# Attention's P V product: the part with v's low half is added into the columns of the high half, and a pair's part is normalised in its PSUM bank

## The chip, the cores and the metric

The kernel runs on one core of a Trainium2 chip. Its engines are TensorE (PE, with its weight loads shown apart as PEld), VectorE (DVE), ScalarE (ACT), GpSimd (POOL) and the issuing queues of SyncE (SP) and ACT for DMAs. The metric is the device time of one execution in microseconds, lower is better; the time before is the median of three runs.

## The reference

Three layers follow each other, all from float32 arrays (weights and inputs are sent as 64-bit numbers and decoded on the chip).

```python
# q, k, v: (4 batches, 8 heads, 576 rows, 64)
q_rot, k_rot = rotate(q), rotate(k)                    # rotary embedding
scores = q_rot @ k_rot^T / 8
attn = exp(scores - rowmax);  attn /= attn.sum + 1e-9
x = (attn @ v), heads side by side                     # (2304, 512)
h = x @ w_in;  x = (h * clip(h + 3, 0, 6) / 6) @ w_out # layer 1, 512 -> 2048 -> 512
h = x @ w2_in; x = (P(h) / Q(h)) @ w2_out              # layer 2, a rational function
```

## The kernel before

Products are made exact enough by splitting a float32 operand into a high and a low half-precision part (layer 2 splits into two float32r parts) and adding the three larger of the four part products.

**Attention.** A batch has eight heads, taken as four pairs (P = 4 b + p). A pair's 576 rows are cut into 128-row chunks 0 to 3 for each head and one chunk 4 of 64 rows of both heads: nine chunks a pair, 36 a batch, 144 in all. They are ordered by batch, then by part: part 0 holds chunks 0 and 1 of all four pairs (16 chunks), part 1 chunks 2, 3 and 4 of all four pairs (20 chunks). For one chunk, `chunk` writes these steps: scores on PE (line 762, PSUM tile `s`), row maximum on DVE (766), its scaling on DVE or POOL (767), exponential on ACT (772, tile `e`), the high half of P (776) and the low half (779, 780) into tile `p` (three buffers), a DMA transpose on SP's queue into `pt` (784, three buffers), and then the product with v on PE (792).

v's tile `v9` of a pair has for each of five row blocks the high half with a column of ones beside it (65 columns, z = 0) and the low half with a column of zeros (65 columns, z = 1). A product is nine matmuls: the five blocks with P's high half (four and the last, shared one) take all 130 columns, the four blocks with P's low half only the first 65. The 64-row chunk does this once for each head. So the result in PSUM has a high part and a low part side by side. Its place is one of the two banks `ob0` and `ob1`, by turns from chunk to chunk. DVE adds the two parts (lines 801 and 804, a reduction over two) into the SBUF tile `xua` (part 0) or `xub` (part 1).

When a pair's part is complete, `x_out` normalises it: a sum with 1e-9 and a reciprocal on DVE (817, 818), the multiply (820, tile `xn`) on POOL or DVE as the planner chooses, the split into `xh` and `xl` (824, 825), and two DMA transposes into `xt` (828), the input of layer 1.

The banks' other columns hold small results (`small`, column 264 or 392 on): sums of squares for scaling, by turns in the two banks. One of them is the transpose of v's maxima in `scale_v` (line 663), which starts the scaling of a batch's v: a maximum (665), a matmul with ones (667), and `pow2` (524, 526, 528), and then `prep_v` writes v's high half (679, on POOL or ACT) and low half (681, DVE).

**Layer 1** (`layer1`) is called for each batch and part. Its 16 hidden blocks (line 859) and four output tiles (line 883) take PSUM tiles `h` from a ring of two; each output tile is copied out by ACT. **Layer 2** starts when attention is over. Its weights are decoded earlier, in the gaps of attention (`prep_w2`).

**What sets the order.** Nothing is issued as it is written. Each step is an `op` with the engines it may run on, an estimated cost, the tiles that it reads and writes, and a priority in ticks (one chunk is a tick; the table `PR` shifts each kind of step). `Plan.order` goes through planned time, and at each moment gives each free engine the ready step of the highest priority; the order that comes out is what each engine gets, and an engine takes its instructions in that order. Tiles with one tag form a ring: they are used in the order in which they were made,

```python
            for n, t in enumerate(ts):
                o = t.ops[0]
                if n:
                    first.append((ts[n - 1].ops[0], o))
                if n >= t.bufs:
                    for x in t.ops:
                        x.deps.update(y for y in ts[n - t.bufs].ops if y is not x)
```

so the first step on a tile comes after the first step on the tile before it, and after all steps on the tile whose buffer it takes. The main loop writes the chunks of a batch in order; after chunk (4, 0) of each pair it calls `scale_v` (at the first pair), `prep_qk` and `prep_v` of the next batch, and after the last pair of a part `layer1` of that part.

Of the kernel before, what the change touches and what calls it, by code (L numbers as in the profile page):

```python
# [10 lines left out]
F32 = mybir.dt.float32  # L11
# [5 lines left out]
ALU = mybir.AluOpType  # L17
AX = mybir.AxisListType
# [5 lines left out]
D = 64  # L24
D2 = 2 * (D + 1)
HP = 4
NB = 9
# [5 lines left out]
LSH = 7  # L33
# [206 lines left out]
def two(e):  # L240
    return float(2.0 ** e)
# [167 lines left out]
def c_dve(n, ap=0):  # L409
    return n * 1.042 + 68 + 60 * ap  # L410
# [27 lines left out]
def attention_moe_moe2(ctx, tc, q, k, v, w1i, w1o, w2i, w2o, a, b, tabs, out):  # L438
# [4 lines left out]
    vec, act, pool, pe, sp = nc.vector, nc.scalar, nc.gpsimd, nc.tensor, nc.sync  # L443
    DE = {"Q": sp, "A": act}
    EL = {"D": vec, "G": pool, "A": act}
# [12 lines left out]
    op, tl = pl.op, pl.tile  # L458

    def EN(key):  # L460
        return PR.get(key + "0", PR[key]) if pl.early else PR[key]
# [25 lines left out]
    obank = [tl("psa", [128, 512], F32, f"ob{i}") for i in range(2)]  # L487
    xu0 = [tl("attn", [128, 2, 2, D + 1], F32, f"xua{i}") for i in range(2)]
    xu1 = [tl("attn", [128, 3, 2, D + 1], F32, f"xub{i}") for i in range(2)]
# [12 lines left out]
    for i in range(2):  # L502
        op("D", 140, lambda e, i=i: vec.memset(xu1[i]()[64:128, 2], 0.0), w=[(xu1[i], "0")])
# [5 lines left out]
    def small(m, n, kind=0):  # L509

        i = nsmall[kind]
        nsmall[kind] += 1
        c = 264 + kind * 128
        t = obank[i % 2]
        return (t, c), lambda: t()[0:m, c:c + n]
# [133 lines left out]
    def scale_v(b_):  # L649
# [10 lines left out]
        for p in range(HP):  # L660
            bound((am, p), lambda p=p: am()[:, p:p + 1], t, 640, 1.4143, lambda p=p: t()[:, 2 * p:2 * p + 2])
        ps, ps_ap = small(HP, 128)
# [5 lines left out]
           r=[ones, m4], w=[p2])  # L668
# [77 lines left out]
    def chunk(i):  # L746
        P, part, cc, h, n = order[i]
        qt, kt, k2, al = prep[P]
        v9 = v9s[P]
        s = tl("psa", [128, 1024], F32, "s", 2)  # L750
# [5 lines left out]
        def mm(e):  # L756
# [12 lines left out]
           r=[(mx, 0), (al, 1)], w=[(mx, 1)])  # L769
        et = tl("attn", [128, S], F32, "e", PR["e"])  # L770
        c0 = cc - 2 * part
# [11 lines left out]
        pt = tl("attn", [128, NB, 128], F16, "pt", PR["pt"])  # L783
        op("Q", (625, 1008, 1), lambda e: DE[e].dma_start_transpose(out=pt(), in_=p16()), r=[p16], w=[pt])
        ob = obank[i % 2]
        vs = [(h, 0, 128, 0)] if cc < 4 else [(0, 0, 64, 0), (1, 64, 64, D2)]

        def pv(e):
            for hh, q0, m, o0 in vs:
                for n_, j in enumerate((0, 1, 2, 3, 5, 6, 7, 8, 4)):  # L790
                    c = D2 // 2 if j > 4 else D2
                    pe.matmul(ob()[0:m, o0:o0 + c], lhsT=pt()[:, j, q0:q0 + m],  # L792
                              rhs=v9()[:, hh, j % 5].rearrange("p s d -> p (s d)")[:, 0:c],
                              start=(n_ == 0), stop=(n_ == NB - 1))
        pl.prio += PR["pv"] * PR["tick"]
        op("P", (c_pe(D2, 5) + c_pe(D + 1, 4)) * len(vs), pv, r=[pt, v9], w=[(ob, 0)])
        xu = (xu0, xu1)[part][n % 2]

        def ev(e):
            if cc < 4:  # L800
                vec.tensor_reduce(out=xu()[:, c0, h], in_=ob()[:, 0:D2].rearrange("p (s d) -> p d s", s=2),
                                  axis=AX.X, op=ALU.add)
            else:
                vec.tensor_reduce(out=xu()[0:64, c0],
                                  in_=ob()[0:64, 0:2 * D2].rearrange("p (h s d) -> p h d s", h=2, s=2),
                                  axis=AX.X, op=ALU.add)
        op("D", c_dve(128 * len(vs)), ev, r=[(ob, 0)], w=[(xu, (c0, h))])

    def x_out(P, part, n):

        b_, p = divmod(P, HP)
        m = 2 + part
        if p == 0:
            xts[b_, part] = [tl("attn", [128, HP, m * 128], F16, f"xt{part}{i}") for i in range(2)]
        xu = (xu0, xu1)[part][n % 2]
        r = tl("attn", [128, 3, 2], F32, "r", 2)
        op("D", 75, lambda e: vec.tensor_scalar(r()[:, 0:m], xu()[:, :, :, D], 1e-9 * two(LSH), None, ALU.add), r=[xu], w=[r])
        op("D", 105, lambda e: vec.reciprocal(r()[:, 0:m], r()[:, 0:m]), w=[r])
        xn = tl("attn", [128, 3, 2, D], F32, "xn")
        op(EN("e_xn"), {"G": 1.75 * m * 128 + 125, "D": c_dve(m * 128)}, lambda e: EL[e].tensor_tensor(  # L820
            xn()[:, 0:m], xu()[:, :, :, 0:D], r()[:, 0:m].unsqueeze(3).to_broadcast([128, m, 2, D]), ALU.mult), r=[xu, r], w=[xn])
# [357 lines left out]
```

## Time and profile before

| | us |
|---|---|
| median of 3 runs (lowest, highest) | 1174.5 (1174.15, 1177.13) |
| the profiled execution | 1176.04 |
| its span, first to last instruction | 1174.3 |
| DVE busy | 1012.9 |
| PE busy | 978.5 |
| ACT busy | 693.6 |
| POOL busy | 536.2 |

The span is what the trace covers; the execution's own time is a little longer. The first product with v starts at 75.3 us and the last at 696.6 us, layer 1 goes on to 762 us, and layer 2 fills the rest. A busy time is the union of an engine's instructions, and the matmuls' ends are modelled: a matmul is shown for about 0.2 us, while the next one starts much earlier. Which engine limits a stretch is read from the stretch, not from the sums.

### The profile page before, as it was taken

The numbers are of one execution on the slowest core, as the hardware profiler recorded it, in microseconds if no ns is written. First come the engines' busy times: TensorE is split into PE (matmuls) and PEld (weight loads), VectorE is DVE, ScalarE is ACT, GpSimd is POOL, SyncE is SP. The second block draws the span as 40 slices with busy tenths as digits, with TensorE's granted clock in tenths as the row PEclk, the third lists the DMA queues.
The fourth block names the chain that finished last, engine by engine and source line by source line (L and its number), as shares of the span: only waits on it lengthen the run. The fifth ranks groups of instructions, "written<-read, shape, count | busy, mean of one in ns | idle before, by whom it ended". The sixth has DMA issues, their size and how long they took to land.

```text
span 1174.3 us, 20041 instructions
## 1 busy us (share of the span) xinstructions
PE 978.5 (83%) x7030; PEld 756.6 (64%) x7030; DVE 1012.9 (86%) x1920; ACT 693.6 (59%) x1274; POOL 536.2 (46%) x603
## 2 busy tenths in 40 slices
PE   0222469887888889988899999989999999999997
PEld 0111247755566666666666787767888888888885
DVE  7999989799899998899978955489988887888787
ACT  5555668475455354453444526478776675676576
POOL 5799778687588857699843620035000000000000
PEclk9999989999999999899999999999999999999999
DMA  8788877787887897978869651622020020010010
GB/s 237 184 219 178 218 145 156 152 175 163 189 177 157 154 220 187 191 149 161 188 165 196 145 127 33 197 83 76 1 61 3 19 54 1 5 41 1 1 37 18
DMA packets 297445, 142.73 MB, mean 122 GB/s; under 512 B 245120, under 2 KB 278528, under 8 KB 297344
## 3 DMA queue, kind: packets, MB, share of 16 engines
q1 hardware_dynamic: 286352, 123.72, 48.8%
q10 hardware_dynamic: 10992, 17.73, 5.3%
q8 instruction: 55, 0.90, 0.3%
q14 instruction: 46, 0.38, 0.1%
HBM read 61.71 MB, written 17.83 MB: 68 GB/s over the span
## 4 chain that ended last, share of the span: by engine, by line
PE 42%; DVE 28%; DMA 8%; issue 6%; POOL 6%; ACT 4%; SPq 1%; ACTq 0%; DVEq 0%; POOLq 0%
PE ac L1079 14%; PE hh L1046 8%; PE hx L1046 7%; PE h L883 6%; PE h L859 5%; DMA pt<-p 4%; DVE mx L766 3%; DVE gl L868 2%; DVE p L453 2%; DVE t L865 2%; DMA w2d<-f 2%; DMA raw<-in_moe_w_out_dram 2%; DVE qk L732 1%; ACT e L772 1%; PE s L762 1%
## 5 line engine op out<-in xcount | busy, mean ns | idle before, releaser
L859 PE MATMUL h<-xt,w 128*128 128x256 f16 (+1 forms) x1536 | 207.6, 289 | 31.8 <-DVE t L865 27.4
L859 PEld LDWEIGHTS <-w 128*128 128x128 f16 x1536 | 149.2, 99 | 73.9 <-issue 36.9
L883 PE MATMUL h<-gh,w 128*128 128x256 f16 (+1 forms) x960 | 195.8, 290 | 0.5 <-DVE w L574 0.4
L772 ACT ACTIVATE e<-s,mx,qal 128x576 f32<-128x576 f32 x144 | 118.7, 827 | 122.8 <-DVE mx L767 37.5
L1079 PE MATMUL ac<-w,lgh 128*128 128x512 f32 x576 | 180.1, 393 | 4.8 <-ACT lgh L1069 4.0
L779 POOL TENSOR_TENSOR p<-e,p 128x512 f16<-128x512 f32 x104 | 138.9, 1335 | 64.6 <-DVE p L453 42.5
L883 PEld LDWEIGHTS <-w 128*128 128x128 f16 x1440 | 139.5, 99 | 36.3 <-DVE w L574 0.7
L883 PE MATMUL h<-gl,w 128*128 128x256 f16 (+1 forms) x480 | 139.2, 290 | 0.0
L762 PE MATMUL s<-t,t 128*128 128x512 f16 (+2 forms) x320 | 89.6, 313 | 55.1 <-ACT e L772 48.2
L792 PE MATMUL ob<-v,pt 128*128 128x130 f16 (+3 forms) x1440 | 96.3, 217 | 45.2 <-DMA pt<-p 19.3
L762 PEld LDWEIGHTS <-t 128*128 128x128 f16 (+1 forms) x640 | 59.0, 108 | 107.2 <-issue 68.4
L1079 PEld LDWEIGHTS ac<-w,lgh 128*128 128x128 f32 x576 | 106.8, 188 | 30.6 <-ACT lgh L1069 6.6
L1046 PE MATMUL hh<-x,w 128*128 128x512 f32 (+1 forms) x516 | 115.9, 373 | 2.9 <-DVE lt L1061 2.9
L792 PEld LDWEIGHTS <-pt 128*128 128x128 f16 (+1 forms) x1440 | 81.5, 105 | 55.4 <-issue 26.4
L1079 PE MATMUL ac<-w,lgl 128*128 128x512 f32 x288 | 113.6, 394 | 1.2 <-DVE lgl L1070 1.2
L766 DVE TENSOR_REDUCE mx<-s 128x1 f32<-128x576 f32 x144 | 107.0, 745 | 6.8 <-PE s L762 6.6
L1046 PEld LDWEIGHTS hh<-x,w 128*128 128x128 f32 x516 | 90.9, 188 | 23.0 <-DVE lt L1061 3.8
L1046 PE MATMUL hx<-x,w 128*128 128x512 f32 (+1 forms) x444 | 98.2, 370 | 0.0
L863 ACT ACTIVATE t<-h,half,d 128x256 f32<-128x256 f32 (+1 forms) x128 | 74.7, 585 | 26.9 <-PE h L859 25.7
L1046 PEld LDWEIGHTS hx<-x,w 128*128 128x128 f32 x444 | 77.4, 188 | 16.1
L868 DVE TENSOR_TENSOR gl<-t,gh 128x256 f16<-128x256 f32 (+1 forms) x108 | 69.2, 643 | 12.1 <-ACT gh L449 11.0
L449 ACT ACTIVATE gh<-t 128x256 f16<-128x256 f32 (+1 forms) x95 | 41.6, 440 | 51.1 <-DVE t L865 48.8
(151 smaller groups left out, 2088.8 us busy)
## 6 DMA issues: line engine op xcount, KB each, us to landing
raw<-in_moe_w_in_dram SPq DMA_DIRECT2D x32, 512.0 KB, 4.8
raw<-in_moe_w_out_dram SPq DMA_DIRECT2D x32, 512.0 KB, 4.5
w2d<-f ACTq DMA_DIRECT2D x30, 256.0 KB, 3.7
w2s<-w2d SPq DMA_DIRECT2D x22, 256.0 KB, 2.7
out_dram<-ob SPq DMA_DIRECT2D x36, 128.0 KB, 2.4
nat<-in_k_dram SPq DMA_DIRECT2D x16, 256.0 KB, 3.2
nat<-in_q_dram SPq DMA_DIRECT2D x16, 256.0 KB, 3.2
vnat<-in_v_dram SPq DMA_DIRECT2D x4, 1024.0 KB, 7.6
```

The source lines that it names most:

```text
L449: act.activation(out, in_, AF.Copy, scale=scale)
L762: pe.matmul(s()[r0:r0 + m, c:c + n_], lhsT=qq[:, q0:q0 + m], rhs=kk[:, k0:k0 + n_], start=(j == 0), stop=(j == 1))
L766: op("D", c_dve(576), lambda e: vec.reduce_max(mx()[:, 0:1], s()[:, 0:S], axis=AX.X), r=[s], w=[(mx, 0)])
L772: op("A", c_act(576, 2, False), lambda e: act.activation(et(), s()[:, 0:S], AF.Exp, bias=mx()[:, 1:2], scale=al()[:, 0:1]), r=[s, (mx, 1), ...
L779: EL[e].tensor_tensor(p16()[:, S + 64:2 * S], et()[:, 0:512], p16()[:, 0:512], ALU.subtract)
L792: pe.matmul(ob()[0:m, o0:o0 + c], lhsT=pt()[:, j, q0:q0 + m], rhs=v9()[:, hh, j % 5].rearrange("p s d -> p (s d)")[:, 0:c], start=(n_ == 0 ...
L859: pe.matmul(hp()[:, 0:N], lhsT=w[:, z, kk], rhs=xt()[:, kk, 0:N], start=(n == 0), stop=(n == 11))
L863: op("A", c_act(N, 2, False), lambda e, t=t, hp=hp, f=f: act.activation(t()[:, 0:N], hp()[:, 0:N], AF.Relu, bias=half(), scale=d()[:, f:f ...
L868: op(EN("e_gl"), c_sub(N), lambda e, t=t, f=f: EL[e].tensor_tensor(gl()[:, f, 0:N], t()[:, 0:N], gh()[:, f, 0:N], ALU.subtract), r=[t, (gh ...
L883: pe.matmul(yp()[:, 0:N], lhsT=w[:, s_, m * 128:(m + 1) * 128], rhs=gt()[:, f, 0:N], start=(f == 0 and z == 0), stop=(f == KF - 1 and z == 2))
L1046: pe.matmul(hp()[:, 0:n], lhsT=w[:, kk], rhs=xt()[:, kk, 0:n], start=(i == 0), stop=(i == 11))
L1079: pe.matmul(accs[j][i]()[0:m], lhsT=gt()[:, x:x + m], rhs=wt(), start=(f == 0 and z == 0), stop=(f == KF - 1 and z == 2))
```

## The change

The product's matmuls with v's low half get their own instruction, 64 columns wide, and write to the columns of the high half, so that PSUM adds the two: 14 narrow matmuls (five blocks twice, four blocks once) in place of nine. The bank is chosen by part (2 P + part is odd for part 1) instead of by chunk, and each chunk and head of a pair's part has its own 65 columns in it, up to 390. The two reductions and their SBUF tiles are gone. `x_out` reads the sums and the values from the bank; its multiply is now given to DVE only. Rows 64 to 127 of the 64-row chunk's columns, which no product writes, are set to 1 once. The small results move to columns 400 and 464 on; the transpose of v's maxima, 128 columns wide, takes a tile of layer 1's ring `h`.

```diff
--- before.py
+++ after.py
@@ -485,8 +485,6 @@
     pw = tl("const", [128, 3], F32, "pw")
     pwi = tl("const", [128, KF], F32, "pwi")
     obank = [tl("psa", [128, 512], F32, f"ob{i}") for i in range(2)]
-    xu0 = [tl("attn", [128, 2, 2, D + 1], F32, f"xua{i}") for i in range(2)]
-    xu1 = [tl("attn", [128, 3, 2, D + 1], F32, f"xub{i}") for i in range(2)]
     v9t = [tl("attn", [128, 2, 5, 2, D + 1], F16, f"v9{i}") for i in range(HP)]
 
     def cosb():
@@ -500,7 +498,7 @@
     op("D", 140, lambda e: vec.memset(ones(), 1.0), w=[ones])
     op("D", 70, lambda e: vec.memset(half(), two(-16)), w=[half])
     for i in range(2):
-        op("D", 140, lambda e, i=i: vec.memset(xu1[i]()[64:128, 2], 0.0), w=[(xu1[i], "0")])
+        op("D", 140, lambda e, i=i: vec.memset(obank[i]()[64:128, 4 * (D + 1):6 * (D + 1)], 1.0), w=[(obank[i], 0)])
     for i in range(HP):
         for z, x in enumerate((1.0, 0.0)):
             op("D", 70, lambda e, i=i, z=z, x=x: vec.memset(v9t[i]()[:, :, :, z, D:D + 1], x), w=[(v9t[i], f"1{z}")])
@@ -510,7 +508,7 @@
 
         i = nsmall[kind]
         nsmall[kind] += 1
-        c = 264 + kind * 128
+        c = 400 + kind * 64
         t = obank[i % 2]
         return (t, c), lambda: t()[0:m, c:c + n]
 
@@ -659,7 +657,10 @@
         op(PR["q_vnat"], (1700, 4300), load, w=[t])
         for p in range(HP):
             bound((am, p), lambda p=p: am()[:, p:p + 1], t, 640, 1.4143, lambda p=p: t()[:, 2 * p:2 * p + 2])
-        ps, ps_ap = small(HP, 128)
+        ps = tl("psh", [128, 512], F32, "h", 2)
+
+        def ps_ap():
+            return ps()[0:HP, 0:128]
         op("P", 110, lambda e: pe.transpose(ps_ap(), am(), ident()), r=[ident] + [(am, p) for p in range(HP)], w=[ps])
         m4 = tl("attn", [HP, 1], F32, "vm4", 2)
         op("D", 200, lambda e: vec.reduce_max(m4(), ps_ap(), axis=AX.X), r=[ps], w=[m4])
@@ -782,29 +783,17 @@
         op(en, {"D": 740, "G": 1380}, lo, r=[et, (p16, 0)], w=[(p16, 1)])
         pt = tl("attn", [128, NB, 128], F16, "pt", PR["pt"])
         op("Q", (625, 1008, 1), lambda e: DE[e].dma_start_transpose(out=pt(), in_=p16()), r=[p16], w=[pt])
-        ob = obank[i % 2]
-        vs = [(h, 0, 128, 0)] if cc < 4 else [(0, 0, 64, 0), (1, 64, 64, D2)]
+        ob = obank[(2 * P + part) % 2]
+        vs = [(h, 0, 128, (2 * c0 + h) * (D + 1))] if cc < 4 else [(0, 0, 64, 4 * (D + 1)), (1, 64, 64, 5 * (D + 1))]
 
         def pv(e):
             for hh, q0, m, o0 in vs:
                 for n_, j in enumerate((0, 1, 2, 3, 5, 6, 7, 8, 4)):
-                    c = D2 // 2 if j > 4 else D2
-                    pe.matmul(ob()[0:m, o0:o0 + c], lhsT=pt()[:, j, q0:q0 + m],
-                              rhs=v9()[:, hh, j % 5].rearrange("p s d -> p (s d)")[:, 0:c],
-                              start=(n_ == 0), stop=(n_ == NB - 1))
+                    for z in range(2 if j < 5 else 1):
+                        pe.matmul(ob()[0:m, o0:o0 + D + 1 - z], lhsT=pt()[:, j, q0:q0 + m], rhs=v9()[:, hh, j % 5, z, 0:D + 1 - z],
+                                  start=(n_ == 0 and z == 0), stop=(n_ == NB - 1 and z == 1))
         pl.prio += PR["pv"] * PR["tick"]
         op("P", (c_pe(D2, 5) + c_pe(D + 1, 4)) * len(vs), pv, r=[pt, v9], w=[(ob, 0)])
-        xu = (xu0, xu1)[part][n % 2]
-
-        def ev(e):
-            if cc < 4:
-                vec.tensor_reduce(out=xu()[:, c0, h], in_=ob()[:, 0:D2].rearrange("p (s d) -> p d s", s=2),
-                                  axis=AX.X, op=ALU.add)
-            else:
-                vec.tensor_reduce(out=xu()[0:64, c0],
-                                  in_=ob()[0:64, 0:2 * D2].rearrange("p (h s d) -> p h d s", h=2, s=2),
-                                  axis=AX.X, op=ALU.add)
-        op("D", c_dve(128 * len(vs)), ev, r=[(ob, 0)], w=[(xu, (c0, h))])
 
     def x_out(P, part, n):
 
@@ -812,13 +801,16 @@
         m = 2 + part
         if p == 0:
             xts[b_, part] = [tl("attn", [128, HP, m * 128], F16, f"xt{part}{i}") for i in range(2)]
-        xu = (xu0, xu1)[part][n % 2]
+        ob = obank[(2 * P + part) % 2]
+
+        def ov():
+            return ob()[:, 0:2 * m * (D + 1)].rearrange("p (j h d) -> p j h d", j=m, h=2)
         r = tl("attn", [128, 3, 2], F32, "r", 2)
-        op("D", 75, lambda e: vec.tensor_scalar(r()[:, 0:m], xu()[:, :, :, D], 1e-9 * two(LSH), None, ALU.add), r=[xu], w=[r])
+        op("D", 75, lambda e: vec.tensor_scalar(r()[:, 0:m], ov()[:, :, :, D], 1e-9 * two(LSH), None, ALU.add), r=[(ob, 0)], w=[r])
         op("D", 105, lambda e: vec.reciprocal(r()[:, 0:m], r()[:, 0:m]), w=[r])
         xn = tl("attn", [128, 3, 2, D], F32, "xn")
-        op(EN("e_xn"), {"G": 1.75 * m * 128 + 125, "D": c_dve(m * 128)}, lambda e: EL[e].tensor_tensor(
-            xn()[:, 0:m], xu()[:, :, :, 0:D], r()[:, 0:m].unsqueeze(3).to_broadcast([128, m, 2, D]), ALU.mult), r=[xu, r], w=[xn])
+        op("D", {"D": c_dve(m * 128)}, lambda e: vec.tensor_tensor(
+            xn()[:, 0:m], ov()[:, :, :, 0:D], r()[:, 0:m].unsqueeze(3).to_broadcast([128, m, 2, D]), ALU.mult), r=[(ob, 0), r], w=[xn])
         xh = tl("attn", [128, 3, 2, D], F16, "xh")
         xl = tl("attn", [128, 3, 2, D], F16, "xl")
         op(EN("e_xh"), c_copy(m * 128), lambda e: copy(e, xh()[:, 0:m], xn()[:, 0:m]), r=[xn], w=[xh])
```

## Rows read from the trace of the kernel before

**Rows 1.** The page: span, and busy time, share and instructions of each engine.
```profile
span 1174.3 us, 20041 instructions
...
PE 978.5 (83%) x7030; PEld 756.6 (64%) x7030; DVE 1012.9 (86%) x1920; ACT 693.6 (59%) x1274; POOL 536.2 (46%) x603
```

**Rows 2.** Busy us of each engine by stretch; x is instructions, then clock, DMA.
```profile
60.00:580.00 520.00, 394.92 (x3649) 294.50 (x3648) 484.99 (x963) 284.71 (x527) 414.02 (x477) 0.98 0.83 175
580.00:700.00 120.00, 113.21 (x1097) 87.59 (x1097) 97.86 (x230) 53.32 (x92) 56.06 (x70) 0.99 0.74 164
700.00:770.00 70.00, 68.43 (x479) 50.81 (x477) 31.99 (x59) 37.85 (x68) 1.75 (x2) 1.00 0.35 111
```

**Rows 3.** Chain of waits: by engine over the span; by line after 700 us.
```profile
PE 42%; DVE 28%; DMA 8%; issue 6%; POOL 6%; ACT 4%; SPq 1%; ACTq 0%; DVEq 0%; POOLq 0%
...
by line: PE ac L1079 34.9%; PE hh L1046 18.6%; PE hx L1046 16.5%; PE h L883 6.5%; PE h L859 5.5%; DVE lt L1068 2.4%; DVE lt L1066 2.2%; DVE lq L1058 2.1%; DVE lq L1065 2.0%; DVE lgl L1070 1.6%; DVE lt L1060 1.4%; issue 1.4%; DVE lt L1061 0.
```

**Rows 4.** Groups by line and shape: count | busy us, mean ns | idle before.
```profile
L801 DVE TENSOR_REDUCE xua<-ob 128x65 f32<-128x130 f32 x64 | 18.0, 282 | 3.3 <-PE ob L792 3.0
L801 DVE TENSOR_REDUCE xub<-ob 128x65 f32<-128x130 f32 x64 | 17.8, 279 | 2.0 <-PE ob L792 2.0
L804 DVE TENSOR_REDUCE xub<-ob 64x130 f32<-64x260 f32 x16 | 6.6, 411 | 4.6 <-PE ob L792 4.6
L820 POOL TENSOR_TENSOR xn<-xub,r 128x384 f32<-128x384 f32 x14 | 13.6, 972 | 8.7 <-DVE r L818 8.6
L820 POOL TENSOR_TENSOR xn<-xua,r 128x256 f32<-128x256 f32 x9 | 7.2, 804 | 11.9 <-DVE r L818 11.1 <-ACT w L449 0.6
L865 DVE SCALAR_TENSOR_TENSOR t<-t,h 128x256 f32<-128x256 f32 x64 | 26.0, 407 | 0.7 <-ACT t L863 0.6
```

**Rows 5.** PE in order of time: start us, us shown, matmuls merged.
```profile
434.55 0.57 PE L792 MATMUL ob<-v,pt 128*128 128x130 f16 x9
434.96 3.60 PE L859 MATMUL h<-xt,w 128*128 128x320 f16 x24
...
445.12 0.19 PE L762 MATMUL s<-t,t 128*128 128x64 f16 x1
445.15 0.19 PE L762 MATMUL s<-k,t 128*128 128x64 f16 x1
```

**Rows 6.** Waits from 60 to 700 us: total us, times, longest us.
```profile
PE ob L792 <- DMA pt<-p: 19.3, 16, 3.0
PE ob L792 <- DVE xua L801: 4.0, 2, 2.3
...
SPq L784 <- PE ob L792: 37.9, 28, 5.2
```

**Rows 7.** In order of time: first and last bank hand-over of the 24.
```profile
88.19 0.26 DVE L801 TENSOR_REDUCE xua<-ob 128x65 f32<-128x130 f32 x1
...
96.58 0.68 PE L792 MATMUL ob<-v,pt 128*128 128x130 f16 x5
...
684.92 0.41 DVE L804 TENSOR_REDUCE xub<-ob 64x130 f32<-64x260 f32 x1
684.93 0.57 PE L792 MATMUL ob<-v,pt 128*128 128x130 f16 x9
685.60 0.15 DVE L817 TENSOR_SCALAR r<-xub 128x6 f32<-128x6 f32 x1
...
686.90 0.54 DVE L820 TENSOR_TENSOR xn<-xub,r 128x384 f32<-128x384 f32 x1
```

**Rows 8.** PE in order of time around batch 2's first product.
```profile
315.06 0.27 PE L663 MATMUL ob<-ident,vam 128*4 128x128 f32 x1
...
396.31 0.58 PE L792 MATMUL ob<-v,pt 128*128 128x130 f16 x9 [1.24 <-DMA pt<-p]
...
400.72 0.27 PE L883 MATMUL h<-gh,w_s 128*128 128x256 f16 x1
```

## The prediction

> **What bounds the kernel now.** I read the page's first part, then the busy time by stretches of the span, then the chain of waits, then the single instructions that the change touches. The page says that VectorE (DVE) is the busiest engine, 86% of the span against 83% for TensorE (PE) [rows 1]. An average over the span hides that there are two halves. By stretches [rows 2], from 60 to 580 us DVE is busy 485.0 of 520 us (93%) while PE is busy 394.9 (76%); from 580 to 700 us PE is busy 113.2 of 120 (94%) and DVE 97.9; from 700 us on PE has 68.4 of 70, and there is no attention work left. So attention, which is all that the change touches, runs where DVE is fullest, and hands over to a stretch where PE is.
>
> The chain of waits puts 28% of the span on DVE, 329 us of 1174.3; after 700 us DVE's lines add up to 2.4 + 2.2 + 2.1 + 2.0 + 1.6 + 1.4 = 11.7% of 474 us, 55 us [rows 3]. That leaves 274 us of chain on DVE up to 700 us. DVE is busy 485.0 + 97.9 = 583 us between 60 and 700. Of a DVE microsecond in attention about 274/583 = 0.47 lies on the chain. The rest is beside other work.
>
> **The change part by part.** *The reductions go.* 128 of them over one head and 16 over the 64-row chunk cost 18.0 + 17.8 + 6.6 = 42.4 us of DVE [rows 4]. All lie before 700 us.
>
> *The normalising multiply goes to DVE.* The edit names DVE alone, where the planner chose between GpSimd (POOL) and DVE; 23 of the 32 are on POOL now, 14 of 384 and 9 of 256 elements, 13.6 + 7.2 = 20.8 us of POOL [rows 4]. On DVE the 384-element one took 0.54 us from SBUF [rows 7]. None reads PSUM here; the nearest row that does is line 865, 256 elements with one operand in PSUM, 0.41 us [rows 4], so I take the SBUF price for PSUM. DVE gains 14 x 0.54 + 9 x 0.41 = 11.3 us. From the other side, if each cost what POOL takes now, it would be 20.8. The sum and the reciprocal ahead of it stay on DVE; the sum reads four or six PSUM elements instead of SBUF ones, bounded by 0 and by a whole reduction more, 0.28 x 32 = 9 us; I take nothing, since its element count is far below the reduction's 130.
>
> DVE's net: 42.4 - 11.3 = 31 us less. At 0.47 that is 14.6 us of the chain; bounds 0 (all hidden) and 31 (DVE sets the pace throughout). I take 14.
>
> *PE runs 14 matmuls instead of 9 in each product*, 800 more in all, with 800 more weight loads. A group of nine starts at 434.55 and the next group at 434.96 [rows 5]: 0.41 us. Two 64-wide matmuls of line 762, each with its own weight load, start 445.12 and 445.15, 0.03 us apart [rows 5]. So four 65-wide ones are 0.12 us, the five 130-wide ones 0.29 or 0.058 each, and 14 narrow ones 14 x 0.03 = 0.42: the same as now. Times 160 groups, 1.6 us, taken as nothing. The upper bound is a group whose 14 steps all take 0.058, 0.81 us, or 64 us more of PE; the lower is a gain of some 3 us. The cover is PE's idle 125 us before 580; after that there is none.
>
> The Trainium skill, "TensorE: Matmul & The Clock Gate", section "LDWEIGHTS (loading the stationary operand)", speaks against this: it gives a weight load as its columns over 1.2, 107 ns for 128, and "Back-to-back issue gap" says that both instructions of a pair set the spacing. By an estimate from that page five more pairs a group would be 0.53 us, 85 us of PE. The trace does not agree for these shapes: nine pairs in 0.41 us.
>
> *The bank is handed over.* A batch's four pairs of one part now follow each other in the same bank, where chunks alternated between two. Inside a pair nothing waits any more: the next chunk has its own columns. But the first product of the next pair waits for sum, reciprocal and multiply of the one before. There are 32 such ends; 8 change part and so bank, 24 do not. The last of the 24 [rows 7]: DVE reads the product at 684.92, sums at 685.60, and ends the multiply at 687.44, 1.84 us after the sum began; with the reduction gone the sum takes its place, and the multiply ends at 686.76. The next product began at 684.93, so it is 1.8 us late. The first of the 24 goes the other way: reduction at 88.19, next product at 96.58 [rows 7], no wait. Worked like this, 12 of the 24 are late, by some 1.5 us each: 18 us of late products. Queued behind a waiting product on PE is a layer-1 group or the next scores, and behind those ACT's exponentials; its transposed P stays in its buffer, and the transposes on SP's queue stand behind that: they wait for products 37.9 us now, 28 times [rows 6].
>
> What speaks for a small price: the same kind of wait stands in the kernel today (a product waits for the reduction two chunks back), 142 times, and PE stood still for it only twice, 4.0 us [rows 6], because the order written out by the planner puts other matmuls ahead. I take 5 us, with 0 and 18 as ends. On DVE the waiting read becomes rarer: 32 sums wait for a product, not 144 reductions.
>
> *v's maximum moves into the ring of layer 1's PSUM tiles.* Tiles of a ring are used in the order in which they are made. scale_v of the next batch is called at the end of the first pair of part 1, after layer 1 of part 0 was laid out, so its transpose can only come after the fourth output tile of that layer 1 has begun and the third is copied out. For batch 2 it now runs at 315.06; that fourth tile begins at 400.72, and the batch's first product was at 396.31 [rows 8]. From the transpose on there are seven steps on PE, DVE and POOL (maximum, sum, three small ones, v's high half, v's low half), each behind a running instruction (DVE's average is 583/1193 = 0.49 us, POOL's 470/547 = 0.86 [rows 2]), two of them about 1 us themselves: an estimate of 8 to 9 us. So the first product comes at about 410, 14 us late; batch 3 repeats this, somewhat milder (11), batch 1 has slack. The scores, exponentials and splits don't need v: a chunk takes 640/144 = 4.4 us, so 14 us is three chunks, and three buffers of split P and three of transposed P can hold them. I take 3 us for both together; the ends are 0 and 25.
>
> *The rest* is free: two memsets change their place at the start, the small results move to other columns, and two tiles leave SBUF.
>
> The sum: -14 + 5 + 3 + 0 = -6 us. The profiled execution took 1176.0 us, 1.7 beyond its span; it becomes 1170.0. It was 1.5 above the median of the runs, 1174.5, so the median becomes 1168.5. The planner works out the whole order anew, so each engine's order from 60 to 700 us can shift; that has no row, and the ranges hold it.
>
> **The rivals.** *All of the 31 us comes through*: DVE at 93% from 60 to 580 speaks for it; against it PE's 94% after 580, and that only 0.47 of DVE's time is on the chain. With the two small waits hidden: about 1174.5 - 25 = 1150.
>
> *The relief is hidden anyway*: what is late next is PE waiting for transposed P, 19.3 us today [rows 6], and the full PE after 580. A faster DVE then waits for both; 1174.
>
> *The hand-over decides (slower).* PE is in order. If the planned place of a next pair's product is right after the multiply, any lateness of DVE stops PE with everything behind it. The price: 18 us of late products, and as much again where late products hold transposed P and SP's queue, less the 14: +22, less what overlaps, about 1185. It decides as soon as a hand-over costs more than 14/24 = 0.6 us on average. For it: DVE is nearly full, so sum, reciprocal and multiply each queue. Against it: PE's 4.0 us now.
>
> *Late v decides (slower).* If the pipeline ahead of the products is full already, batches 2 and 3 lose the whole 14 and 11 us: -14 + 5 + 25 = +16, about 1190. Against it the six buffers.
>
> *Weight loads set the pace (slower).* 64 us of PE, half of it uncovered: 1200. The skill's figure above would make it more; the rows speak against it.
>
> **How the numbers follow.** Forecast 0.42, own range 1160 to 1174; everything comes through 0.12; hidden 0.17; hand-over 0.18; late v 0.08; weight loads 0.03. About 0.3%, 3.5 us, is what a measurement can tell from no change, so the border is 1171 and 1178. Faster: 0.36 of the forecast's 0.42, and the 0.12, and a little of hidden: 0.50. Within: 0.06 and 0.14 of the next: 0.20. Slower: 0.30. The range 1150 to 1190 leaves out half of the "everything" case (0.06) and what of the slower ones lies above 1190 (0.12).
>
> **What would show it.** DVE between 60 and 700 us is busy about 31 us less and POOL 21 less. PE's busy time is within 5 us of now, and a product's 14 matmuls start within 0.45 us of the next group's. In the waits there is a new one of PE's products for the multiply, near 5 us. v's transposes for batches 2 and 3 stand just past the layer-1 tile that they follow, at about 400 and 557, and the first products of these batches follow some 9 us later; the chunk rate then catches up. The last product ends some 6 us earlier and the stretch behind it is as long as now. The prediction is wrong if the wait for the multiply is over 14 us, if the products' spacing is nearer 0.058 than 0.03 us, or if DVE's idle time grows by as much as its work shrinks.

## The result and the profile after

The changed kernel takes 1191.61 us (median of four runs, 1190.71 to 1192.21), the kernel before 1174.33 us on the same chip (1174.09 to 1177.13): a ratio of 1.0141, interval 1.0123 to 1.0159. It is 17 us slower, where 6 us faster was forecast. The profiled execution took 1191.01 us, with a span of 1189.2.

The first part of the page of the changed kernel answers to [rows 1]:

```profile
span 1189.2 us, 21476 instructions
...
PE 987.6 (83%) x7830; PEld 765.6 (64%) x7830; DVE 1010.9 (85%) x1862; ACT 675.7 (57%) x1237; POOL 478.6 (40%) x554
```

DVE lost 144 reductions, yet its busy time fell by 2.0 us and its instructions by 58. ACT lost 18 us and POOL 58. Work went onto DVE that was elsewhere before.

Busy time by stretch (columns as in [rows 2]: PE, PEld, DVE, ACT, POOL, then granted clock and DMA), of the changed kernel:

```profile
60.00:580.00 520.00, 393.27 (x4159) 295.45 (x4158) 474.35 (x898) 260.85 (x477) 348.41 (x418) 0.89 0.86 183
580.00:700.00 120.00, 110.53 (x1231) 83.89 (x1229) 103.79 (x235) 59.15 (x103) 64.32 (x76) 1.00 0.68 131
700.00:770.00 70.00, 67.85 (x561) 52.01 (x560) 28.89 (x56) 30.93 (x57) 1.74 (x2) 1.00 0.40 110
```

Fixed stretches hide a delay, since each kernel is then at another point of its work. Layer 2's first matmul is a better border: everything that the change touches lies ahead of it. In time order on PE, first of the kernel before, then of the changed one:

```profile
743.66 5.74 PE L1046 MATMUL hh<-x,w 128*128 128x512 f32 x24
```
```profile
758.59 5.74 PE L1038 MATMUL hh<-x,w 128*128 128x512 f32 x24
```

It comes 14.93 us later, and behind it 430.6 us are left in both spans. The whole loss lies ahead. The stretch up to that border, first before and then after (columns as above):

```profile
0.00:743.66 743.66, 561.76 (x5110) 419.95 (x5111) 655.50 (x1334) 396.39 (x732) 508.08 (x587) 0.98 0.79 172
```
```profile
0.00:758.59 758.59, 569.21 (x5910) 427.95 (x5911) 654.22 (x1277) 379.15 (x695) 451.11 (x539) 0.93 0.78 168
```

DVE has the same work (1.3 us less) and 16.2 us more idle time (104.4 against 88.2). That is the loss, in the terms of the engine that fills this stretch. What has to be explained is why the relief was not there, and where the idle time came from.

The groups that the prediction priced, of the changed kernel (they answer to [rows 4]; idle time behind the second bar):

```profile
L812 DVE TENSOR_TENSOR xn<-ob,r 128x384 f32<-128x384 f32 x16 | 8.8, 549 | 0.1
L812 DVE TENSOR_TENSOR xn<-ob,r 128x256 f32<-128x256 f32 x16 | 6.6, 413 | 0.1
...
L780 DVE TENSOR_TENSOR p<-e,p 128x512 f16<-128x512 f32 x52 | 44.4, 854 | 2.5 <-ACT p L449 1.9
```

The multiply from PSUM costs 0.549 and 0.413 us, as priced. But the low half of P, which may run on POOL or DVE, runs 52 times on DVE now. In the kernel before it was 40 times:

```profile
L779 DVE TENSOR_TENSOR p<-e,p 128x512 f16<-128x512 f32 x40 | 35.4, 885 | 1.1 <-ACT p L449 0.6
```

The planner used the room on DVE.

The waits from 60 to 700 us (they answer to [rows 6]):

```profile
PE ob L793 <- DMA pt<-p: 29.5, 10, 16.2
...
PE ob L793 <- DVE xn L812: 10.7, 9, 3.9
...
SPq L785 <- PE ob L793: 33.2, 24, 3.4
```

The new wait for the multiply is there, 10.7 us. The wait for transposed P grew by 10 us, with one of 16.2.

PE around batch 2's first product, changed kernel, in order of time (answers to [rows 8]):

```profile
403.45 0.27 PE L664 MATMUL h<-ident,vam 128*4 128x128 f32 x1 [0.76 <-ACT t L449]
...
404.96 0.38 PE L668 MATMUL ob<-vm,ones 4*128 4x1 f32 x2
...
407.64 0.38 PE L586 MATMUL ob<-qam,ones 128*128 128x2 f32 x2 [0.88 <-DVE vpi L522]
...
412.45 0.73 PE L793 MATMUL ob<-v,pt 128*128 128x65 f16 x18
```

v's transpose stands at 403.45 and batch 3's at 565.55 (forecast: about 400 and 557); the first products are at 412.45 and 577.80 instead of 396.31 and 555.9. The third line is what the prediction did not see. It is a sum of squares of q and k, line 586, and it waited for `vpi`, a step of v's scaling: both sums use the same column for small results, in turn.

Counted by products, most of the delay was there before batch 2 needed its v. The 73rd of the 160, eight before batch 2's first, first in the kernel before, then in the changed one:

```profile
372.81 1.02 PE L792 MATMUL ob<-v,pt 128*64 128x130 f16 x18
```
```profile
382.25 1.09 PE L793 MATMUL ob<-v,pt 128*64 128x65 f16 x28
```

That is 9.4 us late, though batch 1's first product was level (245.5 us, before 245.2). Batch 2's first product is 16 us late and batch 3's 22, but the last product of all starts at 709.5 us, 12.9 later than before: the two jumps were mostly made up.

### The profile page after: what moved, and what is told of

It is laid out like the page before. It is cut to its first block, busy times and chain, and to the rows that moved or that the text cites. A ratio compares the mean times of both kernels' runs of the same rounds, so it can differ in the third digit from the quotient of the medians.

```text
span 1189.2 us, 21476 instructions
## 1 busy us (share of the span) xinstructions
PE 987.6 (83%) x7830; PEld 765.6 (64%) x7830; DVE 1010.9 (85%) x1862; ACT 675.7 (57%) x1237; POOL 478.6 (40%) x554
## 4 chain that ended last, share of the span: by engine, by line
PE 39%; DVE 12%; DMA 3%; issue 2%; ACT 1%; POOL 1%; ACTq 0%; SPq 0%; DVEq 0%; POOLq 0%
PE ac L1071 15%; PE hh L1038 8%; PE hx L1038 7%; PE h L875 5%; PE h L851 3%; DMA pt<-p 2%; DVE gl L860 2%; DVE mx L767 1%; DVE p L453 1%; DVE t L857 1%; PE ob L793 1%; DMA w2d<-f 1%; PE s L763 1%; DVE lt L1060 1%; DVE lt L1058 1%
## 5 line engine op out<-in xcount | busy, mean ns | idle before, releaser
L780 POOL TENSOR_TENSOR p<-e,p 128x512 f16<-128x512 f32 x92 | 119.2, 1296 | 64.6 <-DVE p L453 42.5
L793 PE MATMUL ob<-v,pt 128*128 128x65 f16 (+1 forms) x2240 | 99.0, 200 | 52.8 <-DMA pt<-p 31.1
L793 PEld LDWEIGHTS <-pt 128*128 128x128 f16 (+1 forms) x2240 | 90.1, 105 | 63.2 <-DMA pt<-p 34.3
L763 PEld LDWEIGHTS <-t 128*128 128x128 f16 (+1 forms) x640 | 56.4, 108 | 97.3 <-issue 49.6
L860 DVE TENSOR_TENSOR gl<-t,gh 128x320 f16<-128x320 f32 (+1 forms) x113 | 76.4, 683 | 14.5 <-ACT gh L449 11.3
L763 PE MATMUL s<-k,t 128*128 128x512 f16 (+2 forms) x320 | 71.1, 312 | 0.0
```

What stands on the lines that cost most here:

```text
L763: pe.matmul(s()[r0:r0 + m, c:c + n_], lhsT=qq[:, q0:q0 + m], rhs=kk[:, k0:k0 + n_], start=(j == 0), stop=(j == 1))
L780: EL[e].tensor_tensor(p16()[:, S + 64:2 * S], et()[:, 0:512], p16()[:, 0:512], ALU.subtract)
L793: pe.matmul(ob()[0:m, o0:o0 + D + 1 - z], lhsT=pt()[:, j, q0:q0 + m], rhs=v9()[:, hh, j % 5, z, 0:D + 1 - z], start=(n_ == 0 and z == 0), ...
L860: op(EN("e_gl"), c_sub(N), lambda e, t=t, f=f: EL[e].tensor_tensor(gl()[:, f, 0:N], t()[:, 0:N], gh()[:, f, 0:N], ALU.subtract), r=[t, (gh ...
```

## The experiments

Each run was compared with the kernel before on the same chip. "Order" means which engine takes each step and in which sequence.

**First round: what of the change costs?** The first run makes the ring tile for v's maxima ahead of layer 1 of part 0, so that v is no longer late.

```diff
# against the changed kernel
-        ps = tl("psh", [128, 512], F32, "h", 2)
+        ps = vring.pop(b_) if b_ in vring else tl("psh", [128, 512], F32, "h", 2)
...
                     if part == 0:
+                        if b_ + 1 < B:
+                            vring[b_ + 1] = tl("psh", [128, 512], F32, "h", 2)
```

> The changed kernel, but the ring tile of v's maxima for the next batch is made before layer 1 of part 0 is laid out, so that it is no longer behind that layer 1's four output tiles; nothing else differs. Late v (my theory now: the products of batches 1 to 3 stand waiting for v's halves, which come only behind the fourth output tile): v's transposes go back to about 115, 315 and 476 us, the 16 us and 22 us gaps before the first products of batches 2 and 3 (397.3 to 412.4, 561.0 to 577.8) shrink to the 6 and 1 us of before, and the time comes down from 1191.6 to 1165 to 1178. Hand-over (products wait for the multiply in the one bank): 1186 to 1192. A new order as such: anything within 10 us of 1191.6.

1196.41 us, 1.0203 (1.018 to 1.0226). Its transposes of v's maxima stand at 120.6, 340.6 and 502.2 us, where the change has them at 237.6, 403.5 and 565.6: v was in time, and the kernel slower still. The second takes the hand-over away: a pair's part has the bank by turns from pair to pair, in place of by part.

```diff
# against the changed kernel, in chunk and in x_out
-        ob = obank[(2 * P + part) % 2]
+        ob = obank[P % 2]
```

> The changed kernel, but a pair's bank is chosen by the pair (P mod 2) and not by the part, so that the next pair's products go to the other bank and need not wait for the multiply of the pair before; v's maxima stay in the ring. Hand-over: PE's waits for the multiply (10.7 us, 9 times) go, and with them the held transposes: 1191.6 to 1175 or less. Late v: the gaps before batches 2 and 3 stay, the time falls by 0 to 5 us, 1186 to 1192.

1183.97 us, 1.0099 (1.0078 to 1.012): some 5 us better than the change, and still 12 us slower than the kernel before. The third puts v's maxima into the ring `h` in the kernel before, and nothing else; the fourth has the edits of the first and second.

```diff
# against the kernel before
-        ps, ps_ap = small(HP, 128)
+        ps = tl("psh", [128, 512], F32, "h", 2)
+
+        def ps_ap():
+            return ps()[0:HP, 0:128]
```

> The kernel before with one piece of the change alone: the transpose of v's maxima takes a tile of layer 1's ring; products, banks and reductions are as before. Late v: v's transposes move to about 230, 402 and 560 us, the first products of batches 2 and 3 come 10 to 20 us late, and the time is 1184 to 1195 against 1174.3. Hand-over: 1172 to 1177. If the buffers of P hid a late v, as my prediction had it: 1174 to 1178.

> Both repairs at once: the ring tile of v's maxima made early and the bank chosen by the pair. What is left of the change then is the narrow matmuls, the missing reductions and the multiply on DVE. Late v: 0 to 5 us below the kernel with the early ring tile alone, and below before: 1158 to 1174. Hand-over: the same as the kernel with banks by pair alone, 1170 to 1175. If DVE's 31 us do not come through at all: 1174 to 1180.

1192.54 us, 1.0169 (1.0152 to 1.0187), and 1197.5 us, 1.0207 (1.0185 to 1.0228). Late v alone seems to cost all of the loss, and yet the kernel with neither late v nor a shared bank is the slowest. Fixed prices for late v and the shared bank can't give that. What the four have in common is that the planner worked out each order anew.

**Second round: the order held, and the order alone changed.** The fifth run shows the planner the steps of the kernel before, so that its order comes out unchanged, and changes only what the steps issue: narrow matmuls, bank by pair, no reductions, the multiply from the bank where it stood, on DVE. v's maxima stay outside the ring, in two halves of 64 columns.

```diff
# against the kernel before
+        pb = obank[P % 2]
...
+                    for z in range(2 if j < 5 else 1):
+                        pe.matmul(pb()[0:m, o0:o0 + D + 1 - z], ...
...
-        op("D", c_dve(128 * len(vs)), ev, r=[(ob, 0)], w=[(xu, (c0, h))])
+        op("D", c_dve(128 * len(vs)), lambda e: None, r=[(ob, 0)], w=[(xu, (c0, h))])
```

> The change in the order of before: the planner is given the steps, costs and tiles of the kernel before, and only what the steps issue is changed: 14 narrow matmuls into a bank chosen by the pair, nothing in place of the reductions, the sum, reciprocal and multiply from the bank and on DVE at the places that the planner had for them; v's maxima are transposed in two halves of 64 columns (one more matmul and two more small reductions a batch), since a bank has no 128 columns left. Order (my theory now: the new steps themselves are a gain, and what costs is that the planner, with other costs and ties, writes another order and puts other work on DVE): DVE's 31 us come through at 0.47, 1155 to 1170. Change itself (narrow matmuls, the bank or the multiply on DVE cost time): 1180 or more. Relief hidden: 1171 to 1176.

1162.49 us, 0.992 (0.9898 to 0.9942). This version beats both kernels. Its profile, the page's first part:

```profile
span 1163.6 us, 21517 instructions
...
PE 984.4 (85%) x7834; PEld 765.3 (66%) x7834; DVE 984.4 (85%) x1807; ACT 693.0 (60%) x1274; POOL 513.6 (44%) x580
```

ACT has the 1274 instructions that it had before, DVE is 28.5 us lighter. Sixth: the same, with 144 reductions over a constant SBUF tile that nobody reads, at the places of the old ones.

```diff
# against the fifth
+            vec.tensor_reduce(out=xsink()[:, 0:n2 // 2], in_=xsrc()[:, 0:n2]..., axis=AX.X, op=ALU.add)
+        op("D", c_dve(128 * len(vs)), spin, ...
```

> The same as the run in the order of before, with 144 reductions of the same size put back at their places on DVE, but over a constant SBUF tile, so that nothing waits for them and they wait for nothing: DVE's work is that of before plus 11 us. Order: if DVE's time is what the order-kept run gains by, this one loses it again: 10 to 16 us above that run, 1170 to 1182. If the gain comes from products that no longer wait for reductions: within 4 us of that run.

1172.43 us, 1.0008 (0.9995 to 1.0022). The whole gain goes back: it was DVE's relief. Seventh and eighth change nothing but the order of the kernel before: ten of the planner's shifts by half a tick each (such as `z_ob` from 4 to 4.5), and the reductions' planned cost set to what they take [rows 4].

```diff
# the eighth, against the kernel before
-        op("D", c_dve(128 * len(vs)), ev, r=[(ob, 0)], w=[(xu, (c0, h))])
+        op("D", 280 if cc < 4 else 410, ev, r=[(ob, 0)], w=[(xu, (c0, h))])
```

> The kernel before, every instruction the same in kind and number save the engine that the planner picks: ten of the planner's shifts, drawn at random, are moved by half a tick. Order: the order of before is a good one among many and a neutral move of it costs 6 to 25 us: 1180 to 1197. Change itself: 1171 to 1178.

> The kernel before with one number changed that only the planner reads: the reductions' cost is set to what the trace shows (0.28 and 0.41 us in place of 0.20 and 0.34). No instruction changes. Order: 1180 to 1197, as any redrawn order. Change itself: 1171 to 1178; a planner with the truer cost might even gain.

1185.11 us, 1.0117 (1.0094 to 1.014), and 1193.2 us, 1.0186 (1.0155 to 1.0217). The same computation by the same kinds of instructions costs 13 and 21 us more in another order, as much as the change did.

**Third round: the two waits priced in the kept order.** Ninth: the fifth with banks by part. Where the kept order had the next pair's product ahead of the multiply (12 of 24 hand-overs, 14 products), it is moved just behind it. Tenth: the fifth with v's transposes moved behind layer 1's fourth output tile, as the ring does it. Eleventh: both.

```diff
# behind the planner's order; True and False as in the ninth, the other way round in the tenth
+        if True and key[0] == "pv" and key[1] > 0:
+            more.append((marks["xn", key[1] - 1, key[2]], o))
...
+        if False:
+            more += [(marks["y", b_ - 1, 0, 3, 0], marks["vam", b_]), (marks["yc", b_ - 1, 0, 2], marks["vam", b_])]
```

> The order-kept run, but with the change's banks, by part: the products of the next pair that stood ahead of the multiply of the pair before (14 products at 12 of the 24 hand-overs) are moved just behind it in the written order, with what depends on them; all else keeps its place. It prices the hand-over by itself. My prediction's term, 5 us with 0 and 18 as ends: 1163 to 1170 against 1162.5 of the order-kept run. Hand-over rival: 1178 or more.

> The order-kept run with banks by pair, but v's maxima of batches 1 to 3 may only be transposed after the first matmuls of the fourth output tile of layer 1 and after the copy of the third, as the ring makes it; v's halves, the first products of these batches and what depends on them move back in the written order, all else keeps its place. It prices the late v by itself. My prediction's term, 3 us: 1163 to 1168. Late-v rival, 14 and 11 us uncovered: 1180 to 1190.

> Both at once in the kept order: every piece of the change, only the planner's new order is missing. Order theory: the sum of the two prices above the order-kept run, 1165 to 1175, and at least 15 us below the changed kernel's 1191.6. If the pieces cost it: 1185 to 1192.

The ninth took 1170.24 us, 0.9987 (0.9967 to 1.0008): 0.67% or about 8 us more than the fifth. Its waits from 60 to 700 us:

```profile
PE ob L803 <- DVE xn L834: 24.7, 18, 3.5
...
PE ob L803 <- DMA pt<-p: 22.4, 17, 3.1
```

24.7 us of waiting cost 8 us of time. The tenth took 1237.25 us, 1.0565 (1.0535 to 1.0596), 75 us above the fifth, the eleventh 1242.89, 1.0616 (1.0582 to 1.0651). The ninth lies at the edge of what was expected of the prediction's term; the tenth and the eleventh lie far above every expectation, the eleventh by some 68 us above that of the order theory. With every piece of the change in it, the order of before is 51 us slower than the order that the planner wrote for the changed kernel. So the old order is good for the new steps only while v comes in time. The tenth's waits from 60 to 700 us name what happens:

```profile
PEld ob L589 <- ACT junk L583: 56.6, 6, 12.7
PE ob L589 <- ACT junk L583: 56.0, 6, 12.5
...
PE ob L803 <- DMA pt<-p: 29.0, 20, 3.1
```

And in order of time on PE, same kernel:

```profile
396.56 0.38 PE L677 MATMUL ob<-vm,ones 4*128 4x1 f32 x2 [0.61 <-DVE vm L673]
...
405.17 0.58 PE L589 MATMUL ob<-qam,ones 128*128 128x2 f32 x2 [7.92 <-ACT junk L583]
...
422.49 0.59 PE L589 MATMUL ob<-qam,ones 128*128 128x2 f32 x2 [12.51 <-ACT junk L583]
```

The sums for q and k (line 589) stand behind v's sum (677), since each of these small results takes the column that the one before it has left. With v late, the next batch's q and k are late as well, and PE stood 56 us for them.

Thirteenth: the tenth with v's sum in a column of its own, and the q and k sums freed of it.

```diff
# against the tenth
+        p2_ap = lambda t=p2[0]: t()[0:128, 480:481]
```

> The order-kept run with late v as in e10, but the sum of v's maxima gets a column of its own, so that the small results of q and k that follow it in the same column no longer stand behind it. Chain (my theory for e10's 1237 us: v's late sum drags the scaling of the next batch's q and k, 313 to 397 us for the first pair of batch 2): the q and k sums return to about 313, 340, 373 us and the time to 1163 to 1176. If late v itself, by the products that wait, costs it: above 1195.

1176.54 us, 1.0038 (1.0016 to 1.0059): 61 us of the 75 were the chain. Late v itself costs 1.2% over the fifth, 14 us (9 to 19 by the two intervals). The changed kernel with that column, its order worked out anew:

> The changed kernel, planned anew, with the same one mending: the sum of v's maxima in a column of its own. Chain as the cause of the changed kernel's loss: the q and k sums of batch 2 come at 319 to 385 us instead of 319 to 443, and the time falls from 1191.6 by 8 us or more, to 1174 to 1184. Order as such (any order that was not chosen costs 13 to 25 us): 1182 to 1200, without a direction.

1187.5 us, 1.0129 (1.0109 to 1.0149), some 4 us less than unchanged, by the ratios 1.4 us, which the intervals don't tell from nothing. The gain that the chain theory asked for did not come. But the q and k sums of batch 2 hardly moved either (318 to 425 us, against 319 to 443), so the run doesn't price the chain in the changed kernel. Perhaps the planner, which knows of the chain, had already put other work ahead; that is not shown. The twelfth run has the fifth's edits in the seventh's order:

> The same edits as in the order-kept run, but in the order of the half-tick run (1185.1), kept likewise. If the gain belongs to the steps and not to the one order: 0.992 times 1185 = 1176, 1171 to 1180. If it came from the fit to the order of before: 1183 to 1190.

1179.29 us, 1.0072 (1.0048 to 1.0096), where that order without them had 1.0117: 0.45% better, with intervals that just overlap. The edits probably help in that order too, by about half as much.

**Fourth round: the same instructions, another order.** Fifteenth: the changed kernel with bank by pair and v's maxima in halves, that is with the fifth's instructions, planned anew. Sixteenth: its 784 steps that have a choice of engines tied to the engines of the kernel before, the sequence free. Seventeenth: the fifteenth with 120 of the numbers in `PR` moved, until the planner's own length equals that for the kernel before.

```diff
# the sixteenth, against the fifteenth
+        if len(engs) > 1:
+            engs = ENGS[self.nflex]
+            self.nflex += 1
```

> The changed kernel, planned anew, with banks by pair and v's maxima in two halves outside the ring: the same instructions as in the order-kept run (1162.5), only the order is what the planner writes for them. Order: 1175 to 1200, that is 12 us or more above the order-kept run. If late v and the hand-over were all that was wrong with the changed kernel: 1160 to 1170.

> The kernel with everything mended and planned anew (1187.1), but each of the 784 steps that may run on more than one engine is tied to the engine that the order of before gave it; the planner is free in the sequence only. Engine choice as the cause (the planner fills DVE again with 33 steps net that ACT and POOL had): DVE's busy time is back at 984 us and the time at 1165 to 1176. Sequence as the cause: DVE at 984 us, but 1180 to 1200.

> The same kernel with everything mended, engines free, and the planner's shifts moved (122 of them) until its own planned length was as short as that of before. If an order for the new steps can be found in this way: 1160 to 1172, below before. If a planned length says little about the chip: anything from 1165 to 1195.

1187.1 us, 1.0124 (1.01 to 1.0149); 1178.58, 1.0047 (1.0032 to 1.0062); 1181.88, 1.007 (1.0052 to 1.0089). The fifteenth and the fifth consist of the same steps and share the banks in the same way, and in neither does v wait for the ring. They differ by 24.6 us. The page's lines of the fifteenth, then of the sixteenth:

```profile
PE 987.5 (83%) x7834; PEld 766.2 (65%) x7834; DVE 1014.9 (86%) x1847; ACT 679.3 (57%) x1243; POOL 500.6 (42%) x571
```
```profile
PE 985.4 (84%) x7834; PEld 765.7 (65%) x7834; DVE 983.3 (84%) x1807; ACT 691.3 (59%) x1274; POOL 500.7 (43%) x580
```

Planned anew, DVE is as full as it was before the change (1014.9); with the engines tied it is not (983.3). Of the 784 steps 63 went from ACT to DVE and 40 from POOL to DVE, 37 and 33 the other way: 33 more on DVE. Tying them gives 8.5 us back (1187.1 to 1178.6; 9 by the ratios). The other 16 us (1178.6 to 1162.5; 15 by the ratios) are sequence alone. The stretch up to layer 2's first matmul, of the fifth, the fifteenth and the sixteenth (columns as above):

```profile
0.00:731.05 731.05, 565.15 (x5915) 427.78 (x5915) 627.08 (x1222) 395.59 (x731) 485.73 (x564) 0.98 0.80 174
```
```profile
0.00:752.76 752.76, 568.20 (x5914) 428.77 (x5915) 657.62 (x1261) 381.34 (x700) 472.71 (x555) 0.97 0.78 169
```
```profile
0.00:744.48 744.48, 567.44 (x5914) 429.28 (x5915) 626.00 (x1221) 393.14 (x730) 472.90 (x564) 0.98 0.80 171
```

The fifth and the sixteenth have equal DVE work (627.1 and 626.0); the sixteenth's DVE is idle 14.5 us longer (118.5 against 104.0). The fifteenth is idle least of the three (95.1 us) but has 30.5 us more to do.

## Why the prediction was wrong, point by point

**The steps that failed** are two, and each is large enough to turn the forecast's sign.

The first is the sentence "The planner works out the whole order anew, so each engine's order from 60 to 700 us can shift; that has no row, and the ranges hold it." It was given neither a term of the sum nor a rival. Where the runs hold the order, the edits without the two waits gain 0.8% (0.992). Where the planner is free, the same instructions lose 1.24% (1.0124). The swing of 2%, 24 us, is larger than each term of the sum. It is also not particular to this change: two new orders for the kernel before, with no edit of a product, cost 1.2% and 1.9%, and moving v's maxima alone 1.7%. Of every order worked out anew here (eleven of them, the changed kernel's and the mended ones among them) none was as good as the one of before.

The second is the 3 us for late v. In the kept order it measured 14 us by itself, and 75 with what hangs on it. With the measured prices of that order in the sum, and without the chain, it reads -9 + 8 + 14 = +13 us. So the change as written is slower in the old order too, even without the chain.

How the 17 us divide between the two is not shown, since the changed kernel has both at once. For the order speak the first, fourth and fifteenth run, which are slow with v in time, and the 73rd product, which is 9.4 us late before batch 2's v matters.

For the new order there was a number to be had. `order` also works out how long its plan takes (`self.length`): 1015.2 us for the kernel before and 1028.9 for the changed one, 13.8 us more. Of the eleven new orders ten are planned 6.6 to 14.7 us longer than the old one, and all ten are slower. The size doesn't follow: the fourth is planned 7.4 us longer and measured 2.1% slower, the sixteenth 14.1 us longer and 0.5% slower.

**DVE's relief.** The prices held: 42.4 us of reductions gone, the multiply at 0.549 and 0.413 us. In the kept order DVE's busy time falls by 28.5 us, close to the 31, and the time by 9.4 us, a share of 0.33 where the chain of waits gave 0.47. The dummy reductions give the price from the other side: 9.9 us of time for 42.6 us of instructions, by which DVE's busy time grew 21.8 us (part of them lies beside other records), so between 0.23 and 0.46. The -14 was too large by some 5 us; that the fifth run beats the kernel before at all speaks against the rival by which the relief stays hidden. But in the changed kernel the relief was not there to share: DVE's busy time fell by 2.0 us, since the planner filled the freed engine again. The prediction used "DVE between 60 and 700 us is busy about 31 us less" as its first sign; the measured fall there is 4.7 us (485.0 + 97.9 to 474.4 + 103.8), and POOL's 57 where 21 were foretold. Its last sign of being wrong did appear: up to layer 2, DVE's idle time grew by 16.2 us while its work shrank by 1.3.

**The narrow matmuls** cost little, near the forecast; no run has them alone. Two products in a row on PE, changed kernel, and what follows them:

```profile
307.45 1.05 PE L793 MATMUL ob<-v,pt 128*128 128x65 f16 x28
308.34 0.30 PE L875 MATMUL h<-gh,w_s 128*128 128x320 f16 x1
```

28 matmuls in 0.89 us, 0.445 us a product against 0.41 [rows 5] and within the 0.45 foretold. The 0.035 us more make 5.6 us of PE for 160 products, where the prediction worked out 1.6 and took nothing. PE's busy time rose by 9.1 us, not within 5 as foretold; the ends of matmuls are modelled.

**The hand-over** was taken as 5 us with ends at 0 and 18. In the kept order it is about 8 us (0.67%; the intervals of the two runs, 0.9898 to 0.9942 and 0.9967 to 1.0008, leave 3 to 13). In the changed kernel's own order the wait is 10.7 us, below the 14 that was named as the point where the prediction would be wrong, and banks by pair gave 5 us back, with a new order in it. This rival did not decide.

**Late v** was taken as 3 us. The transposes came 3 and 9 us after the places foretold, and the first products 16 and 22 us later than before, where 14 and 11 were expected. The price was wrong, as said above. The reason given, "The scores, exponentials and splits don't need v", does not hold in this kernel: the scaling of the next batch's q and k takes turns with v's in the columns for small results, and the scores need q and k. The rival built on it said about 1190, and 1191.6 came out; but that its number is near is no evidence for it. In the changed kernel, v in time gave 1.0203 and the chain cut gave 1.0129, against 1.0141. Each of these has an order of its own, so the price of late v inside the changed kernel can't be read from a run.

**What stays open.** Which places of the new sequence cost the 16 us was not found. The changed kernel has larger waits for transposed P (29.5 us against 19.3), the fifteenth nearly the old ones (20.4), and both are slow, while the fast fifth has 26.6; no single wait carries it. That the two parts, engines and sequence, add up as 8.5 and 16 rests on one order each. The four rounds also show no measure that foretells a good order: the planner's length told slower orders from the old one, but the seventeenth's, 1014.9 us, was that of the kernel before, and it is 0.7% slower. Nor was it tested why the old order is so good. The shifts in `PR` look sought for the steps of before (`'l1o': 2.503752265906`); an order picked from many for one set of steps would lose by most redraws.

## What to carry to other kernels

Where a program writes the order of the instructions, an edit that adds or drops steps is two changes: what the instructions cost, and a new order. Ask the planner's own length which way the second goes, and price it from the scatter of orders that differ in nothing else (here 13 and 21 us), before believing the first; measure the edit with the order held, and if that gains, keep the order with it. And ask of a relieved engine what the planner will put there: here it took the freed 30 us back.

## What the runs showed of the hardware that was not expected

In the profiled execution of the changed kernel the granted clock was at its lower level (0.50, that is 1.2 of 2.4 GHz) in stretches in which that of the kernel before kept the upper. From 76.2 to 96.7 us, first before, then after:

```profile
76.20:96.70 20.50, 8.13 (x52) 5.24 (x50) 20.33 (x40) 13.05 (x25) 18.63 (x21) 1.00 1.04 234
```
```profile
76.20:96.70 20.50, 8.26 (x86) 5.86 (x82) 20.50 (x35) 10.70 (x21) 15.47 (x18) 0.50 0.81 182
```

PE is busy 8 us of 20.5 in both. Over the span the mean is 0.953 against 0.988. It is not what made the kernel slow. The kernel before itself had different clocks in different executions: on one chip it took 1170.85 us at 0.963, 1172.46 at 0.976 and 1174.98 at 0.989. The sixth run's profiled execution had 0.959 and took 1171.48 us, the fourth's had 0.981 and took 1197.9. In the stretch shown DVE is full (20.50 of 20.50), and PE's matmuls have time.
